# A fused retention and two-layer kernel: the decay of q moved behind the attention, four token blocks loaded ahead of w_in, and a new order of the work

## The chip, the cores and the metric

The kernel runs on one core of a Trainium2 chip. TensorE (PE) multiplies matrices into PSUM, VectorE (DVE) and ScalarE (ACT) do elementwise work, GpSimd (POOL) and SyncE (SP) issue DMA transfers here and compute nothing. The metric is device time in microseconds; three runs of the kernel before took 284.38, 279.27 and 279.20 us, with a median of 279.27 us.

## What is computed

q, k and v have the shape (8 batches, 8 heads, 576 positions, 64), in float32. The attention is a retention: no softmax, but a decay by distance.

```
scores = q @ k.T / sqrt(64)
Dmat   = gamma[h] ** (i - j) for i >= j, else 0        # gamma[h] = 1 - 2 ** (-5 - h)
attn   = (scores * Dmat) @ v
x      = attn, heads side by side                      # (4608, 512)
h      = x @ w_in                                      # (512, 2048)
out    = max(0.01 * h, h) @ w_out                      # (2048, 512)
```

The decay of row i and column j splits into a factor of i, a factor of j and a mask. So the factor of the row may be put on q, or on the row of the result; that of the column goes on v.

## The kernel before

**Blocks and groups.** The 4608 tokens form 36 blocks u of 128 tokens (two chunks of 64) and nine groups g of 512 tokens. A batch has nine chunks, and the decay is counted anew every 256 positions, so a chunk has one of four places in its decay block.

**Attention of one block.** `load` (L348) brings k, q and v as float32 tiles (jobs `ld{u}.1`, `.0` and `.2`; 256 KB each, in two halves where a block crosses a batch). `casts` makes 16-bit copies of them: `ck` is a plain cast (L373). `cq` and `cv` multiply by the decay table, either as one DVE product (L377) or as eight ACT scalings, one for each head (L383). q and k are then turned: for the first eight blocks by PE (`tp`, L413) with a move out of PSUM by DVE or ACT (`yt`, L420), from block 8 on by a transposing DMA on SP's queue (`tr`, L399). `sa` (or `ca`) makes the scores in PSUM (L447), `mk` masks them on DVE (L462), `sb` makes the state sums of k and v (L456), `st` adds them up on DVE (L487 to L493), and `sx` casts the state to 16 bits (L505 to L508). `oa` (or `ca` and `ow`) multiplies masked scores by v and the state by q into the PSUM tile `ot` (L544). `x{u}` casts `ot` into `xT` (L593), the operand of layer 1; in 31 blocks ACT does it and in five DVE.

**The two layers.** Groups 0 and 1 do layer 1 plainly: 16 jobs `h{g}.{f}.{t}` a group (L642, a PSUM bank each) with the leaky relu on ACT (L649). From group 2 on layer 1 is done by seven products of half-size blocks (`a{g}.{n}`, L835) with sums of their results on DVE and copies out of PSUM on ACT or DVE (`cA` L774, `u2` L785, `k5` L788). Layer 2 is done by seven products for all groups (`b{g}`, L913). It needs weight differences that DVE makes once: `wm` of w_out (L688) and `ws` of w_in (L717). PE has four PSUM banks for all these, the pool `acc`.

**What sets the order.** Nothing is scheduled at run time. The string `ORDER` lists every job, and each engine runs its jobs in the order of the list. The table `ENGINE` says which of the castings and copies are DVE's and which ACT's. An item such as `+7@0` stands for seven matmuls of zeros into bank 0 (L982): they compute nothing. They read a tile of zeros, `idle`, that DVE clears at the start (L318).

**The loads.** SP issues k and q of block 0, later k and q from block 12 on and the transposing transfers. All else is issued by POOL, one after the other in the order of the list: the loads, the four blocks of w_in (`wi`, L614, 512 columns each) and the four of w_out (`wo`, L623), which are cast to 16 bits on their way. In the trace, POOL does not issue a transfer before the eighth one ahead of it has landed.

Of the kernel before, what the change touches and what calls it, by code (L numbers as in the profile page):

```python
# [33 lines left out]
class Plan:  # L34
# [52 lines left out]
    for eng, names in {  # L87
        "DVE": """
            ck0 cq0 sx0.0 yt0.0 cq1 sx0.1 cv1 cq2 sx1.0 yt2.1 ck3 cq3 yt3.1 cv3 sx2.1 yt3.0 cq4 cv4 x3 ck5 cq5
            cv5 yt5.1 cq6 sx5 cv6 cq7 ck7 cv7 yt7.0 b0.cA cv8 ck10 sx8.0 cv9 cq9 cq11 cq12 cv10 b1.cA cv13 ck15  # L90
            cv14 cq14 cv15 cq15 sx13.1 sx14 cq16 cv16 cv17 cq17 cq18 a2.3.k5 sx17.0 cv18 sx18 cq19 a3.1.u2 x17
            cv20 ck21 cq21 sx19 a3.2.k5 cq22 cv22 sx20 ck23 cv23 cq23 x20 cv24 cq25 sx23 a4.2.cA cv25 a4.2.u2
            cq26 cq27 cv27 sx25 a5.0.u2 a5.0.k5 cq28 cq29 cv29 ck30 cq30 cv30 ck31 cv31 cq32 sx30 cq33 ck33
            a6.0.cA cv33 cv34 ck34 cq35 cq34 a6.2.cA b5.u2 cv35 a6.3.u2 x32 a7.0.cA x33 a7.0.k5 b5.21 a7.1.cA
            b6.11 b6.u2 a7.3.cA a7.3.u2 a8.0.k5 b7.k5 a8.2.u2 a8.2.k5 b7.21 a8.3.u2 b8.21
        """,
        "ACT": """
            cv0 yt0.1 x0 ck1 ck2 yt1.1 yt1.0 cv2 yt2.0 x1 sx1.1 sx2.0 x2 sx3.0 ck4 sx3.1 yt4.1 yt4.0 ck6 sx4.1
            x4 yt5.0 x5 yt6.0 yt6.1 sx6 yt7.1 sx7 x7 x6 ck8 b0.11 cq8 ck9 b0.u2 cq10 b0.k5 cv11 ck12 sx9 x8 ck11
            cv12 sx10 cq13 b0.21 x9 ck13 sx11 b1.11 sx12 x10 b1.u2 x11 ck14 a2.0.cA b1.k5 a2.0.u2 a2.0.k5 x12  # L100
            a2.1.cA a2.1.u2 x13 a2.1.k5 ck16 ck17 sx15 a2.2.cA a2.2.u2 b1.21 a2.2.k5 sx16 x14 a2.3.cA x15
            a2.3.u2 ck18 b2.cA a3.0.cA b2.11 a3.0.u2 a3.0.k5 a3.1.cA cv19 b2.u2 x16 a3.1.k5 ck19 b2.k5 a3.2.cA
            ck20 cq20 a3.2.u2 cv21 b2.21 ck22 x18 a3.3.cA a3.3.u2 a3.3.k5 x19 b3.cA a4.0.cA b3.11 sx21 ck24
            a4.0.u2 a4.0.k5 cq24 a4.1.cA a4.1.u2 sx22.1 a4.1.k5 x21 b3.u2 ck25 b3.k5 ck26 sx24 a4.2.k5 x22 cv26
            a4.3.cA x23 a4.3.u2 a4.3.k5 ck27 b3.21 a5.0.cA b4.cA ck28 cv28 sx26.0 b4.11 x24 ck29 a5.1.cA a5.1.u2
            a5.1.k5 x25 sx27 sx28 b4.u2 a5.2.cA x26 sx29 b4.k5 a5.2.u2 a5.2.k5 x27 a5.3.cA ck32 a5.3.u2 cv32
            a5.3.k5 cq31 b4.21 x28 x29 sx31.1 a6.0.u2 a6.0.k5 sx32 b5.cA a6.1.cA b5.11 a6.1.u2 x30 a6.1.k5 x31
            a6.2.u2 a6.2.k5 sx33 b5.k5 ck35 a6.3.cA a6.3.k5 sx34 sx35.0 a7.0.u2 b6.cA a7.1.u2 a7.1.k5 a7.2.cA
            a7.2.u2 b6.k5 a7.2.k5 x34 x35 a7.3.k5 a8.0.cA b6.21 a8.0.u2 b7.cA b7.11 a8.1.cA b7.u2 a8.1.k5
            a8.1.u2 a8.2.cA a8.3.cA a8.3.k5 b8.cA b8.u2 b8.k5 b8.11x so8.11x b8.11y  # L110
# [11 lines left out]
    l0.4.256 tp4.0@2 x3 tp5.0@1 yt4.0 st3.1s ld6.1 h0.11.0@0 sx3.1 yt5.0 ld6.2 h0.9.0@2 yt4.1 ck5 cv4 ld7.0
    h0.10.0@1 l0.9.0 tp5.1@3 ld7.2 l0.10.0 ca4 sb4 h0.4.384@2 mk4 ld7.1 cv5 h0.8.0@1 l0.4.384 st4.1 ld8.2 yt5.1 ow4
    sb5 x4 h0.15.0@2 st5.0 sx4.1 st5.1 l0.11.0 h0.14.0@3 sx5 ld8.1 ca5 l0.14.0 cq6 l0.8.0 ld9.2 ws3.1 h0.13.0@0 mk5
    ld9.1 h0.0.128@3 l0.13.0 cv6 wo2 h0.0.384@1 l0.0.128 ld10.2 l0.15.0 tp6.0@0 h0.0.256@3 ck6 yt6.0 ld10.1 tp6.1@2
    l0.0.384 ow5 sb6 wo0 x5 h0.12.0@0 st6.0s yt6.1 ld8.0 h1.0.0@1 cv7 l0.0.256 cq7 ld9.0 h1.2.0@2 l1.0.0 ck7 st6.1
# [88 lines left out]
def kernel(  # L215
# [150 lines left out]
    def casts(u):  # L366
# [5 lines left out]
        def ck():  # L372
            copies[ke](out=by_half(t[:, 1]), in_=in_halves(t32[u, 1][:]))  # L373
# [680 lines left out]
```

## Time and profile before

| | |
|---|---|
| median of three runs | 279.27 us |
| the profiled execution | 281.72 us |
| its span, first to last instruction | 279.9 us |
| granted TensorE clock over the span | 1.000 |
| busy: PE, DVE, ACT, POOL | 269.7, 229.9, 206.6, 72.4 us |
| first layer-1 matmul, first layer-2 matmul, last matmul begins its run | 18.75, 50.80, 275.30 us |

The span is what the profiler saw between the first and the last instruction; 1.8 us of the profiled execution lie around it. In the views a row of a timeline has its start, its length, the engine, the line and the tiles, a count, and in brackets how long the engine stood idle before it and what ended that. A row of a window has the busy time of each engine with the number of its instructions, the clock, the busy share of the DMA engines and the GB/s that they moved. Zero matmuls count as busy.

### The profile page before, as it was taken

What the parts mean: (1) busy time and instruction counts of PE and PEld (TensorE: products, weight loads), DVE (VectorE), ACT (ScalarE), POOL (GpSimd) and SP (SyncE); (2) the same over time, 40 slices, a digit from 0 to 9 for tenths busy, and PEclk for the clock granted to TensorE, in tenths of its full rate; (3) what the DMA queues carried; (4) which work ended last, traced back from release to release, by engine and by line L of the source; (5) the groups of instructions that cost most, each with busy time, mean ns of one, the idle gap of its engine ahead of it and who ended that gap; (6) DMA issues with size and microseconds to landing.
All of it is one profiled execution on the core that took longest, in us unless ns stands there. A gap on an engine that the chain in (4) does not pass through costs nothing.

```text
span 279.9 us, 10117 instructions
## 1 busy us (share of the span) xinstructions
PE 269.7 (96%) x4337; PEld 224.7 (80%) x4337; DVE 229.9 (82%) x431; ACT 206.6 (74%) x459; POOL 72.4 (26%) x92
## 2 busy tenths in 40 slices
PE   7878999899999999999999999999999999999994
...
GB/s 220 238 207 222 275 253 244 260 218 219 213 239 226 213 305 253 155 211 273 277 201 262 187 220 187 148 260 214 21 148 51 68 3 2 152 0 0 77 96 131
DMA packets 94364, 50.04 MB, mean 179 GB/s; under 512 B 83312, under 2 KB 88560, under 8 KB 94320
## 3 DMA queue, kind: packets, MB, share of 16 engines
...
q14 instruction: 10, 0.08, 0.1%
HBM read 36.81 MB, written 9.44 MB: 165 GB/s over the span
## 4 chain that ended last, share of the span: by engine, by line
PE 84%; DMA 11%; POOL 1%; issue 1%; DVE 1%; ACT 0%; POOLq 0%; DVEq 0%
PE acc L913 37%; PE acc L835 32%; PE acc L642 6%; DMA w_in<-in_moe_w_in_dram 6%; PE ot L544 4%; DMA w_out<-in_moe_w_out_dram 4%; PE sc L456 2%; DMA t<-in_k_dram 2%; PE sc L447 2%; POOL t L348 1%; PE sc L913 1%; PE acc L413 0%; DVE w_mix L688 0%; DVE w_out L688 0%; ACT st L505 0%
## 5 line engine op out<-in xcount | busy, mean ns | idle before, releaser
L913 PEld LDWEIGHTS <-gt 128*128 128x128 f16 x720 | 69.8, 98 | 9.5 <-DMA w_out<-in_moe_w_out_dram 0.8
L348 POOL DMA_DIRECT2D t<-in_v_dram x40 | 34.4, 860 | 101.1 <-DVE v L377 63.3
L913 PE MATMUL acc<-w_out,gt 128*128 128x256 f16 x416 | 51.5, 273 | 0.9 <-DMA w_out<-in_moe_w_out_dram 0.9
L835 PEld LDWEIGHTS <-w_in 128*128 128x128 f16 x448 | 42.4, 98 | 5.6
L855 ACT ACTIVATE gt<-acc 128x512 f16<-128x512 f32 x56 | 33.4, 599 | 16.6 <-PE acc L835 16.4
L863 ACT ACTIVATE gt<-sum 128x512 f16<-128x512 f32 x56 | 34.7, 632 | 4.7 <-DVE sum L859 4.7
L913 PE MATMUL acc<-w_mix,gt 128*128 128x256 f16 x288 | 36.2, 273 | 0.0
L835 PEld LDWEIGHTS <-w_sum 128*128 128x128 f16 x336 | 32.2, 98 | 4.1
L835 PE MATMUL acc<-xs,w_sum 128*128 128x256 f16 x224 | 33.6, 273 | 0.0
L835 PE MATMUL acc<-xT,w_in 128*128 128x256 f16 x224 | 33.5, 273 | 0.0
L835 PE MATMUL acc<-xs,w_in 128*128 128x256 f16 x224 | 33.4, 273 | 0.0
L732 POOL DMA_DIRECT2D out_dram<-osb x16 | 11.5, 718 | 83.9 <-ACT acc L774 38.5
L642 PE MATMUL acc<-xT,w_in 128*128 128x256 f16 (+2 forms) x272 | 30.8, 266 | 0.9 <-DMA w_in<-in_moe_w_in_dram 0.7
L913 PEld LDWEIGHTS <-mix 128*128 128x128 f16 x288 | 28.1, 98 | 3.6 <-issue 0.3
L642 PEld LDWEIGHTS <-w_in 128*128 128x128 f16 x272 | 22.0, 98 | 6.0 <-DMA w_in<-in_moe_w_in_dram 0.8
L462 DVE TENSOR_TENSOR s<-sc,cs 128x512 f16<-128x512 f32 x36 | 24.6, 684 | 2.7 <-PE sc L447 1.8
L859 DVE TENSOR_TENSOR sum<-acc,k 128x512 f32<-128x512 f32 x28 | 19.2, 686 | 7.8 <-PE acc L835 5.7
L649 ACT ACTIVATE gt<-acc 128x512 f16<-128x512 f32 x32 | 18.2, 600 | 7.6 <-PE acc L642 7.4
L377 DVE TENSOR_TENSOR qk<-t,cs 128x512 f16<-128x512 f32 x30 | 20.5, 684 | 3.4 <-DMA t<-in_q_dram 3.4
L788 ACT COPY k<-acc 128x512 f32<-128x512 f32 x29 | 16.9, 588 | 7.8 <-PE acc L913 4.0
L593 ACT CAST xT<-ot 128x512 f16<-128x512 f32 x31 | 18.2, 588 | 5.2 <-PE ot L544 5.2
L383 ACT ACTIVATE v<-t,cs 128x64 f16<-128x64 f32 x72 | 18.2, 341 | 3.5 <-DMA t<-in_v_dram 2.9
...
## 6 DMA issues: line engine op xcount, KB each, us to landing
...
```

Of the source, the lines that this page charges most:

```text
L348: engine[eng].dma_start(out=t[CH * j : CH * j + rows], in_=(q, k, v)[x][b, :, CH * w : CH * w + rows, :].rearrange("h t d -> t h d"),)
L377: engine[e].tensor_tensor(out=view[0](out), in0=view[1](t32[u, 2 * x][:]), in1=view[1](decay(u, x)), op=MUL)
L383: nc.scalar.mul(out=out[:, at(h), :], in_=t32[u, 2 * x][:, h, :], mul=tab_sb[:, w, x, h : h + 1])
L462: landed[u] = nc.vector.tensor_tensor(out=s[:], in0=sc[:, :, 0], in1=mask_sb.unsqueeze(1).unsqueeze(1).to_broadcast([P, 2, NP, CH]), op=MUL,)
L593: moved[u] = copies[xe](out=x_of(u).rearrange("q c (j t) -> q j c t", j=2), in_=at)
L642: nc.tensor.matmul(out=a[:, n, :], lhsT=w_in16[:, c, (f0 + n) * P : (f0 + n + 1) * P], rhs=x[:, c, t0 : t0 + nt], start=(n == 0 and c == 0 ...
L649: nc.scalar.activation(out=y[:, f0 : f0 + nf, t0 : t0 + nt], in_=a[:], func=mybir.ActivationFunctionType.Lrelu)
L835: nc.tensor.matmul(out=r[:, f, :], lhsT=w[:, c, (2 * n + f) * P : (2 * n + f + 1) * P], rhs=rhs[:, c, :], start=fresh and c == 0 and f == ...
L855: w = op(what, "ACT", lambda: nc.scalar.activation(out=to(), in_=r[:], func=lr), after, [y], [r])
L859: what, "DVE", lambda: nc.vector.tensor_tensor(out=s[:], in0=r[:], in1=plus[:], op=ADD),
L863: f"l{g}.{n}.{what}", "ACT", lambda: nc.scalar.activation(out=to(), in_=s[:], func=lr), [j], [y],
L913: nc.tensor.matmul(out=(r[tb] if isinstance(r, tuple) else r)[:, tb, :], lhsT=lhs[n]()[:, f, tb * P : (tb + 1) * P], rhs=rhs[n][:, f, :], ...
```

## The change

What it does, by parts:

1. `cq` becomes a plain cast, like `ck`. The row factor comes in at the end: `x{u}` is always a DVE product of `ot` and a table `q_tab`, written to `xT`. `q_tab` is made on the chip at the start by four DVE products (`tb0` to `tb3`) from two short tables, and the table of constants holds the decay of v alone.
2. POOL issues ten loads before the first block of w_in where it issued seven, so that k, q and v of blocks 0 to 3 stand ahead of it. The second and third blocks follow sooner on the first. One load fewer stands ahead of the last block of w_out.
3. `cq8` gets a dependency on `wm2.1`, a weight difference that needs the last block of w_out. The first transposing DMA on SP reads what `cq8` writes.
4. The zeros are read from a part of `w_mix`; the tile `idle` is gone. There are 36 zero matmuls for 33, in other places: 9, 6, 2, 2, 2, 4, 3, 3 and 5, where there were 13, 4, 3, 2, 7, 2 and 2.
5. The state's running sum has a pool of its own with three buffers; the scaling of it works in place.
6. `ORDER` and `ENGINE` are new. On DVE there are now 18 casts of k (12 before), 12 of q, 27 products of v (27), 19 state casts (15), 4 `cA` (8), 7 `u2` (9) and 8 `k5` (7); ACT has the rest. On PE, all attention of blocks 0 to 3 stands ahead of the first layer-1 job; before, that job stood ahead of the outputs of block 2 and the scores of block 3.

```diff
@@ CFG
+    fp=3,
@@ def decay / q_table
-    def decay(u, x):
+    def decay(u):
         w = kinds.index((place(2 * u), place(2 * u + 1)))
-        return tab_sb[:, w, x, :].unsqueeze(2).to_broadcast([P, H, D])
+        return tab_sb[:, w, :].unsqueeze(2).to_broadcast([P, H, D])
+
+    steep = []
+
+    def q_table():
+        for a in range(NB):
+            def run(a=a):
+                nb = CH // FINE
+                nc.vector.tensor_tensor(
+                    out=q_tab[:, a].rearrange("p c (b r) -> p c b r", b=nb),
+                    in0=fine_sb.unsqueeze(2).to_broadcast([P, NP, nb, FINE]),
+                    in1=coarse_sb[:, :, a].unsqueeze(3).to_broadcast([P, NP, nb, FINE]), op=MUL,
+                )
+
+            steep.append(add(f"tb{a}", "DVE", run))
@@ def casts
-        def cq():
-            scaled(t[:, 0], 0, qe, lambda h: 2 * (h % NP) + h // NP, (by_half, in_halves))
...
-        cast[u, 0] = add(f"cq{u}", qe, cq, [loaded[u, 0]], [t], [t32[u, 0]])
+        cast[u, 0] = add(f"cq{u}", qe, lambda: plain(0, qe), [loaded[u, 0]], [t], [t32[u, 0]])
@@ def inner
-                    tmp = t_pool.tile([P, NP, CH], FP, name="stmp")
-                    nc.vector.tensor_tensor(out=tmp, in0=x, in1=before[0][:, before[1]], op=ADD)
+                    nc.vector.tensor_tensor(out=to, in0=x, in1=before[0][:, before[1]], op=ADD)
                     nc.vector.tensor_tensor(
-                        out=to, in0=tmp, in1=gblk_sb.unsqueeze(2).to_broadcast([P, NP, CH]), op=MUL
+                        out=to, in0=to, in1=gblk_sb.unsqueeze(2).to_broadcast([P, NP, CH]), op=MUL
                     )
@@ def outer_copy
-            moved[u] = copies[xe](out=x_of(u).rearrange("q c (j t) -> q j c t", j=2), in_=at)
-
-        copied[u] = add(f"x{u}", xe, cp, [j], [xT[u // 4]], [ot_banks])
+            by_place = (
+                q_tab[:, p0 : p0 + 1].to_broadcast([P, 2, NP, CH]) if p0 == p1
+                else q_tab[:, p0 : p1 + 1 : p1 - p0] if p0 < p1
+                else q_tab[:, p0 : (p1 - 1 if p1 else None) : p1 - p0]
+            )
+            moved[u] = nc.vector.tensor_tensor(
+                out=x_of(u).rearrange("q c (j t) -> q j c t", j=2), in0=at, in1=by_place, op=MUL
+            )
+
+        copied[u] = add(f"x{u}", "DVE", cp, [j] + [steep[p] for p in sorted({p0, p1})], [xT[u // 4]], [ot_banks])
@@ at the start, and behind sum_weights()
-    idle = const_pool.tile([P, TOK], F16, name="idle")
+    idle = w_mix[:, 2, 0:2].rearrange("p f n -> p (f n)")
+    cast[CFG["turned"], 0].after.append(mixed_w[2, 1])
```

**POOL, from its seventh transfer on.** `t_0`, `t_1` and `t_2` are tiles of q, k and v, `w_in` a block of w_in; `x2` is a pair of halves or of like transfers. Before:

```order
L348 DMA t_2_165<-in_v_dram 128x8x64
L614 DMA w_in_123<-in_moe_w_in_dram 128x4x512
L348 DMA t_1_220<-in_k_dram 128x8x64
L348 DMA t_0_226<-in_q_dram 128x8x64
L348 DMA t_1_260<-in_k_dram 64x8x64 x2
L348 DMA t_2_293<-in_v_dram 128x8x64
L348 DMA t_0_326<-in_q_dram 64x8x64 x2
L348 DMA t_0_445<-in_q_dram 128x8x64
L614 DMA w_in_123<-in_moe_w_in_dram 128x4x512
```

and of the change, from the same place:

```order
L363 DMA t_2_221<-in_v_dram 128x8x64
L363 DMA t_2_223<-in_v_dram 128x8x64
L363 DMA t_1_262<-in_k_dram 128x8x64
L363 DMA t_0_312<-in_q_dram 128x8x64
L641 DMA w_in_124<-in_moe_w_in_dram 128x4x512
L363 DMA t_0_324<-in_q_dram 64x8x64 x2
L641 DMA w_in_124<-in_moe_w_in_dram 128x4x512
L363 DMA t_1_359<-in_k_dram 64x8x64 x2
L641 DMA w_in_124<-in_moe_w_in_dram 128x4x512
```

Three loads have moved ahead of the first block of w_in, and the second and third blocks come one pair of halves behind the one before; they had eight and four transfers between, each half counted.

**DVE, from the clearing of the zeros on.** `sc` holds scores and state sums in PSUM, `cs` the table of constants, `s` a masked score or a state, `st` a state in 16 bits. Before:

```order
L318 MEMSET idle 128x256
L373 CAST qk_147<-t_1_135 128x2x4x64
L377 TENSOR_TENSOR qk_147<-t_0_139,cs 128x2x4x64
L377 TENSOR_TENSOR qk_163<-t_0_141,cs 128x2x4x64
L487 COPY s_222<-sc 128x256
L420 COPY qkT<-acc 128x512
L377 TENSOR_TENSOR qk_228<-t_0_149,cs 128x2x4x64
L377 TENSOR_TENSOR v_258<-t_2_152,cs 128x512
L489 TENSOR_TENSOR s_222<-sc,s_222 128x256
L508 CAST st_265<-s_222 128x256
L462 TENSOR_TENSOR s_291<-sc,cs 128x512
```

and of the change, two stretches of the same engine's order, the second one ending with block 3's mask and the x products of blocks 2 and 3:

```order
L333 MEMSET w_mix 128x256
L381 TENSOR_TENSOR q_tab<-cs 128x256 x4
L406 TENSOR_TENSOR v_183<-t_2_139,cs 128x512
L402 CAST qk_188<-t_1_143 128x2x4x64
L508 COPY s_208<-sc 128x256
L510 TENSOR_TENSOR s_208<-sc,s_208 128x256
...
L618 TENSOR_TENSOR xT<-ot,q_tab 128x2x4x64
L510 TENSOR_TENSOR s_483<-sc,s_410 128x256
L483 TENSOR_TENSOR s_485<-sc,cs 128x512
L618 TENSOR_TENSOR xT<-ot,q_tab 128x2x4x64
L483 TENSOR_TENSOR s_550<-sc,cs 128x512
L618 TENSOR_TENSOR xT<-ot,q_tab 128x2x4x64 x2
```

The q products have left the start, the four table products have come ahead of all else, and four x products follow each other closely.

**SP, its first transfers.** `qkT` is the turned q and k, and the transposing rows read blocks 8 and 9. Before:

```order
L348 DMA t_1_135<-in_k_dram 128x8x64
L348 DMA t_0_139<-in_q_dram 128x8x64
L399 DMA_TRANSPOSE qkT<-qk_1048 128x8x128
L348 DMA t_1_1417<-in_k_dram 128x8x64
L348 DMA t_0_1429<-in_q_dram 128x8x64
L399 DMA_TRANSPOSE qkT<-qk_1115 128x8x128
```

and of the change:

```order
L363 DMA t_0_137<-in_q_dram 128x8x64
L363 DMA t_1_141<-in_k_dram 128x8x64
L420 DMA_TRANSPOSE qkT<-qk_1111 128x8x128
L363 DMA t_1_1471<-in_k_dram 128x8x64
L363 DMA t_0_1501<-in_q_dram 128x8x64
L420 DMA_TRANSPOSE qkT<-qk_1106 128x8x128
```

The order is the same but for q and k of block 0; what has changed is that `qk_1111`, the tile of block 8, gets its q only behind the weight difference, and the loads of block 12 stand behind the transfer that reads it.

More of the change, by code (lines that the diff above doesn't have):

```diff
@@ L100 @@
[L100 to L109, printed above, removed]
@@ L122 @@
[L122 to L126, printed above, removed]
@@ new lines @@
+    b1.p5.1 b1.p7.0 ld15.0 x11 xs2.0 xs2.1 a2.0.11 m1.3.1 b1.k5 a2.0.p5.0@2 a2.0.p6.0 mk12 ld16.0 b1.p3.0 a2.0.k5
+    a2.0.p3.0 ld17.0 cv16 xs2.2 a2.0.u2 st13.1 b1.p3.1 ld16.1 a2.0.p7.0 ck14 xs2.3 a2.0.12 cv14 cq14 b1.12 b1.p7.1
+    ow12 sb14 a2.0.22 ld18.2 b1.22 l2.0.22 ca13 a2.1.p1.0@2 ck15 st14.0 b1.p4.0 cq15 cq16 a2.1.cA@0 a2.0.p4.0
+    a2.1.p6.0 l2.0.12 st14.1 mk13 cv15 tr14 a2.0.21 x12 tr15 a2.1.p2.0 a2.1.p5.0@1 sx13.1 a2.1.u2 b1.p4.1 a2.1.p7.0
+    a2.1.k5 a2.1.p3.0 b1.21 a2.2.p1.0@3 sb15 ws4.1 a2.1.22 sx14 a2.1.11 ow13 ca14 a2.1.12 a2.2.p5.0@1 ck16 a2.2.cA@2
@@ L211 @@
+    m8.1.1 b8.p5.1 m8.2.1 m8.3.1 so7.1 m8.3.0 b8.p6.0 b8.k5 b8.p6.1 b8.u2 b8.p2.0 b8.p7.0 b8.11x b8.p7.1 b8.22
+    b8.p3.0 so8.11x so8.22 b8.p3.1 b8.p4.0 b8.12 b8.p4.1 so8.12 b8.21 b8.p2.1 so8.21 b8.11y so8.11y
 """
@@ L248 @@
     kinds = sorted({(place(2 * n), place(2 * n + 1)) for n in range(NU)})
-    tab = np.zeros((P, len(kinds), 2, H))
+    tab = np.zeros((P, len(kinds), H))
     for w, at in enumerate(kinds):
         r = np.concatenate([CH * a + np.arange(CH) for a in at])[:, None] - BLK / 2
-        tab[:, w, 0] = gamma[None, :] ** r * scale
-        tab[:, w, 1] = gamma[None, :] ** (-r)
+        tab[:, w] = gamma[None, :] ** (-r)
+    NB, FINE = BLK // CH, 16
+    fine, coarse = np.zeros((P, NP, FINE)), np.zeros((P, NP, BLK // FINE))
+    for c in range(NP):
+        for oo in range(2):
+            rows = slice(CH * oo, CH * oo + CH)
+            fine[rows, c] = gamma[2 * c + oo] ** np.arange(FINE)
+            coarse[rows, c] = gamma[2 * c + oo] ** (FINE * np.arange(BLK // FINE) - BLK / 2) * scale
     s_idx = np.arange(P) % CH
@@ L275 @@
     a_pool = pool("ap", CFG["ap"])
+    f_pool = pool("fp", CFG["fp"])
     c_pool = pool("cp", CFG["cp"])
@@ L286 @@
     n_pool = pool("np", 4)
-    t_pool = pool("tp", 1)
     sc_pool = pool("scp", 1, PSUM)
@@ L370, in casts, with plain, cv @@
         ke, qe, ve = by(f"ck{u}", "ACT"), by(f"cq{u}", "DVE"), by(f"cv{u}", "DVE")
-        def ck():
-            copies[ke](out=by_half(t[:, 1]), in_=in_halves(t32[u, 1][:]))
-        def scaled(out, x, e, at, view):
-            if e != "ACT":
-                engine[e].tensor_tensor(
-                    out=view[0](out), in0=view[1](t32[u, 2 * x][:]), in1=view[1](decay(u, x)), op=MUL
-                )
+        def plain(x, e):
+            copies[e](out=by_half(t[:, x]), in_=in_halves(t32[u, x][:]))
+        def cv():
+            if ve != "ACT":
+                engine[ve].tensor_tensor(out=s[:], in0=t32[u, 2][:], in1=decay(u), op=MUL)
                 return
```

229 lines of the change are left out of this document (120 added, 109 removed), and 12 rows, old and new, of the table loads.

## The prediction

> **What bounds the kernel now.** I read the page's busy times and slices first, then a table of windows over the start, then the PE timeline and the chain of waits at the places where PE is not full.
>
> ```profile
> span 279.9 us, 10117 instructions
> PE 269.7 (96%) x4337; PEld 224.7 (80%) x4337; DVE 229.9 (82%) x431; ACT 206.6 (74%) x459; POOL 72.4 (26%) x92
> ...
> PE   7878999899999999999999999999999999999994
> ...
> PE 84%; DMA 11%; POOL 1%; issue 1%; DVE 1%; ACT 0%; POOLq 0%; DVEq 0%
> ```
>
> PE is busy for 96% of the span, and PE holds 84% of the chain. The only other large holder is DMA, 11%, and it sits in the first quarter. So time can be won where PE idles or multiplies zeros, in the first 63 us, and lost anywhere an engine begins to starve PE. The windows (PE, PEld, DVE, ACT, POOL, clock, DMA share, GB/s) show where:
>
> ```profile
> 0.00:7.00 7.00, 5.58 (x13) 1.79 (x13) 1.58 (x5) 2.70 (x8) 5.90 (x11) 1.00 0.78 221
> 7.00:14.00 7.00, 6.11 (x124) 3.70 (x125) 5.56 (x13) 5.76 (x18) 6.73 (x9) 1.00 1.04 237
> 14.00:21.00 7.00, 4.95 (x94) 2.92 (x93) 3.83 (x10) 3.13 (x7) 3.32 (x5) 1.00 0.80 206
> 21.00:28.00 7.00, 5.89 (x139) 3.96 (x138) 5.32 (x12) 3.94 (x8) 5.29 (x7) 1.00 1.06 222
> 28.00:35.00 7.00, 7.00 (x134) 4.10 (x132) 4.04 (x10) 4.29 (x9) 4.37 (x6) 1.00 1.15 274
> 42.00:49.00 7.00, 6.86 (x155) 5.72 (x154) 5.28 (x11) 5.91 (x12) 3.99 (x6) 1.00 1.12 245
> 49.00:56.00 7.00, 6.13 (x92) 5.11 (x90) 5.64 (x11) 4.53 (x10) 3.91 (x5) 1.00 1.16 259
> 56.00:63.00 7.00, 6.85 (x64) 6.00 (x62) 6.20 (x12) 4.06 (x12) 0.89 (x1) 1.00 1.17 219
> 71.00:218.00 147.00, 147.00 (x2611) 126.88 (x2610) 139.32 (x268) 127.30 (x284) 27.44 (x34) 1.00 0.94 203
> ```
>
> From 28 us PE is full, but for 0.14 + 0.87 + 0.15 = 1.16 us between 42 and 63. From 71 to 218 it is full without a gap, with DVE at 139.32 of 147. Before 28 us it idles 5.5 us, and part of what counts as busy is zeros. The PE timeline, the POOL timeline and the chain tell what those early stretches wait for:
>
> ```profile
> 1.23 5.58 PE L982 MATMUL acc<-idle 128*128 128x512 f16 x13 [1.23 <-DVE idle L318]
> 18.51 0.40 PE L413 MATMUL acc<-ident,qk 128*128 128x128 f16 x4 [1.77 <-DVE qk L373]
> 18.75 1.04 PE L642 MATMUL acc<-xT,w_in 128*128 128x256 f16 x8
> 19.62 0.59 PE L982 MATMUL acc<-idle 128*128 128x512 f16 x2
> 24.13 0.32 PE L544 MATMUL ot<-s,v 64*64 64x64 f16 x16
> 24.28 0.61 PE L544 MATMUL ot<-qkT,st 64*64 64x64 f16 x16
> 26.10 2.76 PE L642 MATMUL acc<-xT,w_in 128*128 128x512 f16 x12 [0.66 <-DMA w_in<-in_moe_w_in_dram]
> 50.80 1.05 PE L913 MATMUL acc<-w_out,gt 128*128 128x256 f16 x8 [0.67 <-DMA w_out<-in_moe_w_out_dram]
> 55.53 1.03 PE L913 MATMUL acc<-w_out,gt 128*128 128x256 f16 x8 [0.19 <-DMA w_out<-in_moe_w_out_dram]
> ```
>
> ```profile
> 17.33 0.90 POOL L348 DMA_DIRECT2D t<-in_q_dram  x1 [3.60 <-DMA w_in<-in_moe_w_in_dram]
> ...
> 18.03 0.43 DVE L373 CAST qk<-t 128x512 f16<-128x512 f32 x1 [2.98 <-DMA t<-in_k_dram]
> ```
>
> ```profile
> 7.57 9.22 DMA w_in<-in_moe_w_in_dram
> 18.29 7.77 DMA w_in<-in_moe_w_in_dram
> 48.99 10.53 DMA w_out<-in_moe_w_out_dram
> ```
>
> The first w_in block is issued at 7.57, ahead of block 3's q and k, and lands at 16.79. POOL waits 3.60 us for it before it issues more, so the queue of transfers runs dry (share 0.80, 206 GB/s at 14 to 21). Block 3's k lands only at 18, and blocks 2 and 3 finish their attention between matmuls of layer 1. The second w_in block lands at 26.06, and PE starts on it at 26.10. That is the last start-up wait.
>
> **The change, part by part.** *Start.* With four blocks loaded before w_in, the order has all their attention ahead of the first layer-1 job. It is then bounded by DVE. DVE's prices:
>
> ```profile
> L462 DVE TENSOR_TENSOR s<-sc,cs 128x512 f16<-128x512 f32 x36 | 24.6, 684 | 2.7 <-PE sc L447 1.8 <-PE sc L456 0.9
> ...
> L377 DVE TENSOR_TENSOR qk<-t,cs 128x512 f16<-128x512 f32 x30 | 20.5, 684 | 3.4 <-DMA t<-in_q_dram 3.4
> ...
> L489 DVE TENSOR_TENSOR s<-sc,s 128x256 f32<-128x256 f32 x40 | 16.7, 419 | 3.1 <-PE sc L456 2.2 <-PE sc L447 0.8
> ...
> L785 DVE COPY u<-acc 128x512 f32<-128x512 f32 x9 | 6.2, 686 | 2.7 <-PE acc L835 2.7
> ...
> L373 DVE CAST qk<-t 128x512 f16<-128x512 f32 x12 | 5.2, 444 | 6.8 <-DMA t<-in_k_dram 6.8
> L508 DVE CAST st<-s 128x256 f16<-128x256 f32 x7 | 2.5, 352 | 0.0
> ```
>
> Up to block 3's mask DVE now does four products for the q table (4 x 0.419), three scalings of v (3 x 0.684), one cast of k (0.444), eight state sums and two moves of transposed blocks (10 x 0.419), four state casts (4 x 0.352), four masks and two x products (6 x 0.684): 13.9 us; where a form is new or has no row here, the price is that of the nearest row of its size. It can start near 4.3, since the table lies on chip before the product that reads it at 5.15:
>
> ```profile
> 3.93 0.43 DVE L373 CAST qk<-t 128x512 f16<-128x512 f32 x1 [2.76 <-DMA t<-in_k_dram]
> 5.15 0.69 DVE L377 TENSOR_TENSOR qk<-t,cs 128x512 f16<-128x512 f32 x1 [0.80 <-DMA t<-in_q_dram]
> ...
> 30.17 0.68 DVE L377 TENSOR_TENSOR v<-t,cs 128x512 f16<-128x512 f32 x1
> 30.77 0.42 DVE L487 COPY s<-sc 128x256 f32<-128x256 f32 x1
> ```
>
> 4.3 + 13.9 = 18.2 with neither gap nor overlap. The last two rows show starts 0.60 apart for 0.68 of duration, so these 28 instructions overlap by some 2 us, down to 16.0; waits for PE and for transfers add some of it back. I take 17.8. PE's last step of block 3 (the rows at 24.13 and 24.28, 0.8 together) and five zero matmuls (0.59 for two, so about 1.2) follow: the first layer-1 job starts at 19.8. Then PE lacks, against its state at 26.10 before, three layer-1 jobs (0.87 each; the row at 18.75 has 1.04 with its tail) and three transposes (0.25 each): 3.35 us. It stands at 23.1 where it stood at 26.10: **3.0 us sooner**. Bounds: 4.8 (DVE done at 16.0) and nothing (the first w_in block 3 us later than 19.8). With three more loads ahead on POOL, 256 KB at some 259 GB/s each (1.0 us), that block lands near 16.79 + 3.0 = 19.8, just in time, so I keep the middle.
>
> *w_out.* The waits of 0.67 and 0.19 and the hops beside them are the 1.16 us above. They go, and the 3.0 us stay won, if w_out comes sooner by 3.0 + 1.2 = 4.2 us. The last block landed at 48.99 + 10.53 = 59.52. Two things bring it forward. At the mean of the full windows (274, 245 and 259, so 259 GB/s), what the windows from 7 to 28 moved, (237 + 206 + 222) x 7, is 18.0 us of work in 21: 3.0 us of hole that back-to-back loads can close. And 34 loads instead of 35 stand ahead of it: 1.0 us. Both: 4.0 us, landing at 55.5; the second alone: 58.5. I take three quarters of the hole, 56.3, 0.8 to 1.2 us short of all that is wanted at that last block; but 3.5 us more of layer 1 now stands ahead of layer 2's first job, which covers the blocks that land before. I count **1.2 us** of gain with bounds of -1.8 (w_out only 1.0 sooner eats most of the 3.0) and 2.3 (less is lost also in the small steps between).
>
> *DVE and ACT after 71 us.* Before, x was mostly ACT's:
>
> ```profile
> L593 ACT CAST xT<-ot 128x512 f16<-128x512 f32 x31 | 18.2, 588 | 5.2 <-PE ot L544 5.2
> ...
> L593 DVE CAST xT<-ot 128x512 f16<-128x512 f32 x5 | 3.4, 684 | 0.3 <-PE ot L544 0.3
> ```
>
> Between groups 1 and 6 of layer 2 (71 to 218 us) the tables give DVE 23 x products where it had 2 casts of x (+21 x 0.684 = 14.4), 8 q casts where it had 20 q products (3.6 - 13.7 = -10.1), five more k casts (+2.2), three more state casts (+1.3), and fewer v scalings (-1.4) and copies of accumulators (-2.8): +3.6 us. 139.3 + 3.6 = 142.9 of 147: still below PE, price nothing. A product out of PSUM with a broadcast table is what the mask does at 684 ns, and a cast of ot on DVE costs 684 too, so I price x at 684; bounds are 588 and 1368 (a copy and a product one after the other). ACT, at 127.3 of 147, gives up 18.2 us of x casts, takes over q casts in their place, and stays below. The cover is PE's own work; without it the 3.6 us would be paid.
>
> *Held transfer.* Cast 8 of q now waits for a mix of w_out's last block, so the first transposing transfer and two loads behind it on SP start after 56.3 + about 1.5 = 57.8. Before, that transfer started at 57.90:
>
> ```profile
> 57.90 1.94 SPq L399 DMA_TRANSPOSE qkT<-qk  x1
> ```
>
> Price nothing; if w_out lands at 59.5 it is 3 us late, and so are blocks 12 and 13, needed from group 3's layer 1 on, after 100 us. *Zero matmuls* go from 33 to 36 and fill time in which PE has nothing else; only the last five lie in the sum above. The smaller table, the pool of three and the padding change no time that I can see.
>
> Sum: 3.0 + 1.2 = 4.2 us. The profiled execution took 281.72 (span 279.9 and 1.8 around it), so 277.5 in such an execution; the median of the three runs, 279.27, is 2.45 lower, which gives **275.0 us**.
>
> **The rivals.** (1) *The transfers set the start of layer 2* (0.20): for it, the queue is full from 28 us on, and more loads come ahead of w_in. w_out then lands only 1.0 us sooner, PE waits for it, and 1.2 us are won: 278.0. (2) *All of the hole closes* and DVE's chain ends at 16.0 (0.14): 4.8 + 1.7 = 6.5, so 272.8. (3) *DVE becomes the bound, slower* (0.06): if each x product costs 1.37 us, 23 of them add 15.7 to 142.9, 158.6 for a stretch of 147: 11.6 lost less 4.2 won, 286.7. It decides from 4.1 / 23 = 0.18 us over 0.684 on. The mask's row speaks against it. (4) *DVE at 97% is late in small pieces* (0.08): its 3.6 us are paid in full, 278.6. For it: PE has four accumulators of one bank each, so that it waits soon for a late copy. (5) *More casts on DVE hold up POOL's transfers* (0.03): if a cast of k or q on DVE stops POOL for its 0.444 us, the nine that stand before w_out's landing, for five before, bring w_out 1.8 us later: 276.8. The cast at 18.03 ran inside the issue at 17.33, which took 0.90 us like others, so little speaks for it. The Trainium skill ("SBUF — State Buffer", section "Who interferes with whom") has a rule for this: DVE copies and casts can take a port pair that GpSimd needs, and a transfer issued from GpSimd then waits for its descriptors. By that rule this change would pay, since q turns from product to cast; by the pair of rows above it would not.
>
> **How the numbers follow.** The forecast has 0.49; with 273.6 to 276.6 as its own range. The range of 272.3 to 278.6 takes in rivals 1, 2, 4 and 5 and leaves out the DVE-bound case and the tails. A measurement of this kernel can tell about 2%, 5.6 us, from no change: faster is below 273.7, slower above 284.9. Rival 2 and the forecast's lower edge give 0.21 for faster, rival 3 gives 0.05 for slower, and 0.74 stays within.
>
> **What would show it.** Right: the first layer-1 matmul near 19.8 with no layer-1 work ahead of block 3's last attention step, no POOL wait of 3 us between 14 and 18, PE full from 23 to 24 us on, waits for w_out of nearly nothing, DVE near 97% from 67 to 214, x products at 684 ns. Wrong: a wait for w_in or w_out of over 1 us on PE, x products over 0.86 us, or gaps in PE after 71 us.

## The result and the profile after

The changed kernel takes 291.09 us (median of four, 289.81 to 293.84), the kernel before 279.24. The ratio is 1.044, with a 95% interval of 1.035 to 1.053: slower, where 275.0 us were forecast. Where executions of one kernel lie more than 1.5% apart, the ratios here use the faster ones alone, so that a median can lie above what its ratio gives.

The page of the changed kernel, its rows as in the page of before:

```profile
span 289.0 us, 10088 instructions
PE 272.7 (94%) x4340; PEld 226.9 (79%) x4340; DVE 236.8 (82%) x453; ACT 192.3 (67%) x399; POOL 72.7 (25%) x92
...
PE   8889999997699999995999999899999999999995
...
PEclk9999999999699999999999999999999999999999
...
PE 76%; DMA 11%; DVE 7%; ACT 2%; issue 2%; POOL 1%; DVEq 0%; POOLq 0%; ACTq 0%
```

From the fourth slice on (21.7 us) PE's row is full, as forecast. Two holes have appeared where there was none, near 72 and near 130 us, and behind the first one the granted clock is down. DVE's share of the chain of waits has gone from 1% to 7%. The windows show the same holes: from 71 to 218 us, where PE had no gap, it now lacks 8 us. DVE is less busy in that stretch than before, but the stretch also holds less work; over the whole kernel it is busy for 236.8 us, before 229.9.

```profile
14.00:21.00 7.00, 5.70 (x162) 3.51 (x148) 5.44 (x11) 3.54 (x8) 4.20 (x6) 1.00 1.14 218
21.00:28.00 7.00, 6.83 (x70) 4.86 (x68) 3.07 (x7) 4.04 (x8) 5.52 (x8) 1.00 1.15 263
49.00:56.00 7.00, 7.00 (x66) 6.26 (x65) 6.39 (x12) 4.97 (x10) 2.06 (x3) 1.00 1.15 276
71.00:218.00 147.00, 138.89 (x2432) 118.82 (x2432) 130.32 (x257) 109.21 (x233) 25.65 (x32) 0.98 0.91 198
```

The PE timeline names what ended the holes. The rows with L940 between 74 and 82 are runs of eight matmuls, or two such runs (x16): at full clock a run of eight takes 0.87 us from its start to the next.

```profile
20.62 2.80 PE L669 MATMUL acc<-xT,w_in 128*128 128x256 f16 x32
69.05 1.04 PE L940 MATMUL acc<-w_out,gt 128*128 128x256 f16 x8
74.51 0.32 PE L564 MATMUL ot<-qkT,st 64*64 64x64 f16 x6 [3.99 <-DMA qkT<-qk]
74.99 1.89 PE L940 MATMUL acc<-w_out,gt 128*128 128x256 f16 x8
76.67 1.92 PE L940 MATMUL acc<-w_out,mix 128*128 128x256 f16 x8
78.38 3.00 PE L940 MATMUL acc<-w_out,gt 128*128 128x256 f16 x16
81.21 1.04 PE L940 MATMUL acc<-w_mix,mix 128*128 128x256 f16 x8
105.17 1.91 PE L940 MATMUL acc<-w_out,gt 128*128 128x256 f16 x16
133.27 0.25 PE L564 MATMUL ot<-qkT,st 64*64 64x64 f16 x6 [3.30 <-DMA qkT<-qk]
137.09 1.91 PE L940 MATMUL acc<-w_out,gt 128*128 128x256 f16 x16
```

At 74.51 and 133.27 PE had waited for a transposing transfer, of block 10 and of block 20; the rows are the first matmuls of `ca10` and `ca20`. From 74.99 to 81.21 four runs take 6.2 us where they need 3.5: 2.7 us, in which the windows give half the clock:

```profile
72.00:76.00 4.00, 1.49 (x29) 1.15 (x29) 1.24 (x3) 0.00 (x0) 0.01 (x1) 0.72 1.21 204
76.00:80.00 4.00, 4.00 (x21) 2.86 (x19) 2.76 (x6) 3.01 (x10) 0.23 (x1) 0.50 1.23 171
```

SP's queue and the chain of waits show the transfers: block 8's starts where it did in the trace of before (57.85 for 57.90), block 10's is the first of the three at 66.64 and takes 7.83 us, block 20's takes 8.16.

```profile
57.85 1.32 SPq L420 DMA_TRANSPOSE qkT<-qk  x1
...
66.64 7.40 SPq L420 DMA_TRANSPOSE qkT<-qk  x3
```

```profile
66.64 7.83 DMA qkT<-qk
125.06 8.16 DMA qkT<-qk
```

### The profile page after: what moved, and what is told of

Same layout as the page of the kernel before. It is cut to its first block, busy times and chain, and to the rows that moved or that the text cites. A ratio compares the mean times of both kernels' runs of the same rounds, so it can differ in the third digit from the quotient of the medians.

```text
span 289.0 us, 10088 instructions
## 1 busy us (share of the span) xinstructions
PE 272.7 (94%) x4340; PEld 226.9 (79%) x4340; DVE 236.8 (82%) x453; ACT 192.3 (67%) x399; POOL 72.7 (25%) x92
## 4 chain that ended last, share of the span: by engine, by line
PE 76%; DMA 11%; DVE 7%; ACT 2%; issue 2%; POOL 1%; DVEq 0%; POOLq 0%; ACTq 0%
PE acc L940 34%; PE acc L862 26%; PE acc L669 8%; DMA qkT<-qk 6%; DMA t<-in_q_dram 4%; PE ot L564 3%; DMA t<-in_k_dram 2%; PE sc L468 1%; PE sc L477 1%; PE sc L940 1%; DVE sum L886 1%; POOL t L363 1%; DVE mix L916 1%; DVE v L406 1%; DVE s L510 1%
## 5 line engine op out<-in xcount | busy, mean ns | idle before, releaser
L940 PEld LDWEIGHTS <-gt 128*128 128x128 f16 x720 | 70.9, 99 | 10.0 <-DVE gt L916 0.8
L940 PE MATMUL acc<-w_out,gt 128*128 128x256 f16 x416 | 53.4, 279 | 0.0
L940 PE MATMUL acc<-w_mix,gt 128*128 128x256 f16 x288 | 36.2, 273 | 0.5 <-DVE gt L916 0.5
L890 ACT ACTIVATE gt<-sum 128x512 f16<-128x512 f32 x56 | 33.2, 628 | 1.1 <-DVE sum L886 1.0
L862 PE MATMUL acc<-xs,w_in 128*128 128x256 f16 x224 | 32.4, 273 | 0.0
L940 PEld LDWEIGHTS <-mix 128*128 128x128 f16 x288 | 28.5, 99 | 3.9
L402 ACT CAST qk<-t 128x512 f16<-128x512 f32 x42 | 25.6, 619 | 6.3 <-DMA t<-in_q_dram 3.8
L801 ACT COPY acc<-acc 128x512 f32<-128x512 f32 x32 | 18.4, 576 | 13.1 <-PE acc L940 7.0
L618 DVE TENSOR_TENSOR xT<-ot,q_tab 128x512 f16<-128x512 f32 x36 | 24.4, 681 | 1.6 <-PE ot L564 1.6
L812 ACT COPY u<-acc 128x512 f32<-128x512 f32 x30 | 17.5, 588 | 11.3 <-PE acc L940 6.5
```

The source lines that it names most:

```text
L402: copies[e](out=by_half(t[:, x]), in_=in_halves(t32[u, x][:]))
L618: moved[u] = nc.vector.tensor_tensor(out=x_of(u).rearrange("q c (j t) -> q j c t", j=2), in0=at, in1=by_place, op=MUL)
L801: copies[ce](out=B[:], in_=A[:])
L812: op("u2", ue, lambda: copies[ue](out=u2[:], in_=B[:]), [done["6"]], [u2], [B])
L862: nc.tensor.matmul(out=r[:, f, :], lhsT=w[:, c, (2 * n + f) * P : (2 * n + f + 1) * P], rhs=rhs[:, c, :], start=fresh and c == 0 and f == ...
L890: f"l{g}.{n}.{what}", "ACT", lambda: nc.scalar.activation(out=to(), in_=s[:], func=lr), [j], [y],
```

## The experiments

The first theory was this. PE now asks for blocks 10 and 20 before their transposing transfers are in, and each wait costs its length and a few microseconds of half clock behind it. Its rivals were the held-back first transfer, a full set of DMA engines, and DVE. In the expectations theory 2 is the held transfer (or the chain of transfers as a whole); theory 3 is DVE in the first of them and the full DMA engines from e9 on.

**Block 10's scores later on PE** (e1_late10):

```diff
- m1.0.0 ca10 b1.p1.1 ... b1.p5.0@0 m1.1.1 mk10 b1.p2.0 b1.p2.1 ld14.1 b1.p6.0 ow10
+ m1.0.0 b1.p1.1 ... b1.p5.0@0 m1.1.1 b1.p2.0 b1.p2.1 ld14.1 b1.p6.0 ca10 mk10 ... ow10
```

> The scores of block 10 (ca10), its mask and its outputs stand about 4 us of PE work later, behind b1.p6.0; nothing else moves. Theory 1 (PE's order asks for block 10 before its transposing transfer is in, and the clock falls because PE then idles): the wait of 3.99 us and the 2.7 us at a low clock go, so 291.1 - 6.7 = 284.4 us (283 to 286), clock 1.00 from 72 to 84 us. Theory 2 (the whole chain of transposing transfers is late because of the held cq8): the wait moves on to block 11 or 12 and less than 2 us is won, 289 to 291. Theory 3 (DVE bounds the middle of the kernel): no change, 291.

Measured: 286.37 us, ratio 1.026 (1.023 to 1.030). The wait at block 10 and the low clock behind it are gone, but 4.7 us are won instead of 6.7: there are new waits of 0.3 to 0.7 us behind the move, and at block 20 PE waits 3.84 us and the clock falls, which it had not done there. Theory 1 holds for the place and not for the sum.

**The wait filled with matmuls** (e2_filled10):

```diff
- m1.0.0 ca10
+ m1.0.0 +16@0 ca10
```

> Sixteen matmuls that compute nothing (some 3.7 us) stand ahead of ca10, where PE waited 3.99 us. They shorten no wait. If the clock falls because PE stands idle there, it now stays at 1.00 and the 2.7 us lost after the wait come back: 288.4 us (287.5 to 289.5). If the clock falls for another reason, the time stays at 291.

Measured: 284.18 us, ratio 1.013 (1.011 to 1.015). The clock is 1.00 from 70 to 90 us. The traced execution took 287.73 us and another one 288.91, 2 to 3 us less than the change, as expected if the clock falls because PE stands idle; block 20's wait and a low clock behind it remained in the trace. The three fastest executions, on which the ratio rests, had a mean clock of 1.00 and were 7 to 8 us faster than the change. Why those did not dip at block 20 has not been settled.

**The hold undone** (e3_free8):

```diff
-    cast[CFG["turned"], 0].after.append(mixed_w[2, 1])
- b0.p1.1 sx8.0 wm2.1 cq8 wm0.1
+ m0.1.1 l1.10.256 cq8 wm2.0
```

> The hold is undone: cq8 has no dependency on w_out and stands on DVE ahead of wm2.0, some 7 us earlier. Theory 2 (the hold makes the transposing transfers late): the first one starts near 51 instead of 57.85, that of block 10 lands before PE asks for it at 70.5, and the wait and the low clock go: 284.4 us, less 0 to 2 us if w_out now lands later. Theory 1 without the hold as its origin (transfer of block 10 slowed by stores and loads beside it): it still lands after 72 and 288 us or more remain.

Measured: 286.08 us (282.0 to 287.9), ratio 1.014 (1.008 to 1.021). In the traced execution block 10's wait is gone; block 20's is 4.01 us, with a low clock behind it. So the second wait does not come from the hold. That the hold has a part in the first one is not shown by this trace alone: e14 below has no hold and the wait, e5 has the hold and hardly any wait.

**Block 10's transfer ahead of block 13's loads** (e4_turn_first):

```diff
- tr9 ... ld13.1 ... ld13.0 ... tr10
+ tr9 ... tr10 ld13.1 ld13.0
```

> On SP the transposing transfer of block 10 stands ahead of the k and q loads of block 13 instead of behind them; the hold stays. Theory 1: it is issued near 63.8 instead of 66.64 and, at 4 to 5 us, lands by 69, before PE asks at 70.5: 284.4 us. If its 7.8 us come from what runs beside it and not from its place in the queue, it lands near 71.5 and a wait of 1 us and some low clock stay: 287 to 289.

Measured: 288.92 us, with executions from 283.2 to 293.6, too far apart for a ratio. Block 10's wait is gone, and PE waits at block 12 (1.01 us), for copies at 78 and 88 us, and at block 20 (3.34 us). The wait moved along the queue.

**Block 20 later, and with the free cq8** (e5_late20, e6_free8_late20):

```diff
- ow19 ck22 ca20 a3.2.p7.0 ... b3.p1.0@0
+ ow19 ck22 a3.2.p7.0 ... b3.p1.0@0 ca20 mk20
```

> The hold and block 10 are as in the changed kernel; the scores of block 20 and their mask stand 4.4 us of PE work later, behind b3.p1.0. Theory 1 (each wait for a transposing transfer costs its own length and the low clock that follows): 3.3 and about 2.6 us go, 291.1 - 5.9 = 285.2 us (284 to 287); the first wait, at block 10, stays. Theory 2 (the transfers as a chain are behind, and PE meets the next one): a wait of 2 us or more at block 21 or 22, 288 or more.

> Both: cq8 without the hold and earlier, and block 20's scores behind b3.p1.0. Theory 1: no wait for a transposing transfer is left; from the run with the free cq8 (profile 283.0 us in span, 4.2 us of wait at block 20 and 2.5 at the low clock) that leaves a span of 276.5 and a time of about 278 us, between 276.5 and 279, so at or below the 279.5 of the kernel before. If the start's gain of 3 us is real it must show here. Theory 2: 281 or more, with waits at other blocks.

Measured: 286.97 us, ratio 1.026 (1.020 to 1.032), and 290.45 us, ratio 1.034 (1.026 to 1.042). The first won 4 of the 5.9 us, but not by its edit alone. In its trace (285.74 us) block 10's wait is 0.35 us too, though nothing ahead of it differs from the change: that transfer took 4.80 us here, for 7.83. With neither wait and a mean clock of 0.999, this execution is still 6 us longer than the kernel before; PE loses most of them in many waits of 0.3 to 0.9 us, most of them for copies and sums of ACT and DVE. The second, which should have been the best, has a median as high as the change's. In its trace, at 286.88 us its fastest execution, PE waits at blocks 11 and 12 (0.70 and 0.90 us) with the clock at 0.58 from 80 to 84 us, and 1.90 us for a product of DVE near 180 us. Theory 1, taken as two waits that can be removed one by one, falls here.

**One store later; stores cut; the same cut in the kernel before** (e7_free8_store, e9_less_stored, e10_before_less_stored):

```diff
# e7, on top of e3
- ld25.2 ... tr20 so2.0 ... ld26.2
+ ld25.2 ... tr20 ... ld26.2 so2.0
# e9 and e10, groups 0 to 4
-            nc.gpsimd.dma_start(out=out[r0 : r0 + HT, :].rearrange("(t p) d -> p t d", p=P), in_=o[:])
+                nc.gpsimd.dma_start(out=out[r0 : r0 + P, 0:64], in_=o[:, 0, 0:64])
```

> cq8 free as before, block 20 asked for as early as in the changed kernel, but the output store that POOL issues while block 20's transposing transfer is under way (so2.0) is issued later, behind the v load of block 26. If the 8 to 9 us of that transfer come from the store beside it, it lands in 4 to 5 us and the wait is gone: 277 to 279 us. If they come from the loads and the other transposing transfers on SP's own queue, it stays near 8 us: 284 to 286 us.

> The changed kernel, with the output stores of groups 0 to 4 cut to a sixteenth (32 KB of 512 KB each; the other rows and columns of those groups are left out of the output). All else stays. Theory 3 (from 60 us on the DMA engines are full, and a transposing transfer that runs beside a 512 KB store or a load takes 8 to 10 us instead of 3 to 5): the waits at blocks 10 and 20 shrink to under 1 us each and the clock stays up: 280 to 283 us. Theory 1 (PE's order asks too soon whatever runs beside): 288 to 291 us.

> The same cut of the stores in the kernel before, as a control. It waits for no transfer after 60 us, so every theory expects 279.0 to 279.6 us; a gain of over 1 us would say that the cut saves something else than waits for transposing transfers.

Measured: e7 283.55 us, ratio 1.011 (1.004 to 1.018), with block 20's transfer at 7.41 us for 8.89 and its wait at 2.53 for 4.01. e9 284.02 us, ratio 1.009 (1.004 to 1.014), so 7 us less than the change. e10 279.78, ratio 1.001 (0.998 to 1.004). Cutting the stores is worth nothing to the kernel before and more than half of the loss to the changed one. The PE timeline of e9 has one wait of over 0.5 us left after 50 us, and the window from 71 to 218 lacks 2.3 us where the change lacked 8.1:

```profile
72.85 0.32 PE L564 MATMUL ot<-qkT,st 64*64 64x64 f16 x6 [3.23 <-DMA qkT<-qk]
```

```profile
71.00:218.00 147.00, 144.71 (x2545) 124.74 (x2545) 137.02 (x270) 112.99 (x241) 24.09 (x31) 0.99 0.76 166
```

The share of the DMA engines is 0.76 there, for 0.91. Block 10's wait is hardly shorter (its transfer takes 7.23 us), so what slows that transfer is not the stores; block 20's takes 5.31 us, for 8.16.

**The loads alone** (e8_before_loads), the kernel before with three loads ahead of w_in:

```diff
- cq1 ld2.2 +13@3 tp1.0@0 wi1 ... ld3.1 ... ld3.0 ... ld4.1 ... ld3.2
+ cq1 ld2.2 +13@3 tp1.0@0 ... ld3.1 ... ld3.0 ... ld3.2 wi1 ld4.1
```

> The kernel before, with one part of the change alone: the loads of block 3 stand ahead of the first block of w_in on POOL's queue, and PE's order is the old one. If the start's gain comes from the loads alone, PE is full 2 to 3 us sooner and the time is 277 us. If it needs PE's order too (the first layer-1 job now waits for w_in, landing near 19.8, ahead of attention that could run), the time is within 1 us of 279.5 us or 1 us longer.

Measured: 282.07 us, ratio 1.007 (1.003 to 1.011). Nothing is won. One execution took 279.18 us with a mean clock of 1.00; the others had 0.99 and 281.6 to 283.4. The trace shows why, in the window of 4 us behind a wait of 1.81 us for w_in (PE idle for 1.9 of the 4 us before):

```profile
16.00:20.00 4.00, 2.13 (x23) 1.29 (x17) 1.80 (x4) 1.08 (x2) 0.73 (x2) 0.98 1.10 256
20.00:24.00 4.00, 3.88 (x81) 2.67 (x80) 1.62 (x3) 1.05 (x4) 3.91 (x5) 0.59 0.94 227
```

**The decay alone** (e11_old_order): the plain cast of q, the table and x as a DVE product, in the old order, with the old loads.

```diff
- ck0 ld2.0 cq0
+ tb0 tb1 tb2 tb3 ck0 ld2.0 cq0        # all cq on ACT, all x on DVE, no hold
```

> One part of the change alone: q only cast (all casts of q on ACT), the table products, and x as a DVE product, in the order, the loads and the other engine choices of the kernel before; nothing held back. If the decay's move is harmless, DVE has 31 x products for 30 q products, ACT 31 x casts less and 36 q casts for 6 sets of scalings and no more: 278.5 to 281 us. If part of the 12 us comes from it (x late behind DVE's queue, so that layer 1 waits), 284 us or more.

Measured: 288.69 us, ratio 1.029 (1.022 to 1.036), in the traced execution 290.2 us with a span of 288.4. With all casts of q on ACT, this part by itself costs 8 to 9 us in the old order. Layer 2's second group starts at 74.2 us, 5.7 later than in the kernel before, with a low clock from 7 to 14 us; and from 71 to 218 PE lacks 3.3 us in many small pieces while DVE has room:

```profile
7.00:14.00 7.00, 4.57 (x55) 2.34 (x55) 2.00 (x5) 6.06 (x18) 6.70 (x9) 0.76 1.07 260
...
71.00:218.00 147.00, 143.69 (x2558) 122.56 (x2557) 134.47 (x257) 118.97 (x253) 26.67 (x33) 1.00 0.92 201
```

**The start given away** (e12_start_later):

```diff
- oa3 +5@2 h0.6.0@0
+ oa3 +17@2 h0.6.0@0
```

> The changed kernel with twelve zero matmuls more ahead of the first layer-1 job: PE's work starts 3.0 us later, so what the start won is given away. If the transfers set the pace after 60 us (theories 1 and 3), the waits at blocks 10 and 20 shrink by as much and the time stays at 291 us or falls, down to 286 us where the clock then holds. If PE's own work sets it, 294 us.

Measured: 286.93 us, ratio 1.023 (1.017 to 1.030). PE starts layer 1 at 23.0 us for 20.6, and the kernel is 4 us faster. Block 10's wait is 2.20 us for 3.99, block 20's is gone. So PE's own work does not set the pace of the changed kernel there; a later start even helps it.

**Both kernels traced again, and three moves together** (e13_before_again, e15_after_again, e14_three_moves: cq8 as in e3, the store as in e7, and ca20 behind a3.2.p3.0).

> The kernel before, unchanged, traced a second time. The trace behind the prediction had a span of 279.9 us where nearly all other executions have 277.3 to 278.0. If that one execution was long in its start, this trace shows PE 2 to 3 us sooner at the first layer-1 jobs and at layer 2 (68.7 instead of 71.1 us), and the start of the changed kernel is then worth about 1 us and not 3. If the difference lies elsewhere, the start is as it was and the 3 us were real.

> The changed kernel, unchanged, traced a second time: waits of 2 to 4 us at blocks 10 and 20, each followed by some 4 us at about half the clock, and 289 to 294 us. If the waits are elsewhere in this execution, the places named so far are chance, and only their sum (PE ahead of its transfers) is a property of the order.

> The changed kernel with cq8 free and early, the store so2.0 behind the v load of block 26, and block 20's scores 1.7 us of PE work later. Theory 3: the wait at block 10 is gone with the free cq8 and the one at block 20 has shrunk to under 1 us: a span of 278 to 280, 280 to 282 us where the clock holds. If it stays above 283, waits for transfers turn up wherever PE is early, and no single move repairs it.

Measured: e13 279.12 us with a span of 277.3, as expected of it. In its POOL and PE timelines the wait for w_in is 2.64 us instead of 3.60, the first zeros take 4.44 us instead of 5.58, and layer 2's second group starts at 68.52 instead of 71.12; the other rows give the same place in later groups, and SP's transfers for blocks 10 and 20 with PE's use of them:

```profile
1.23 4.44 PE L982 MATMUL acc<-idle 128*128 128x512 f16 x13 [1.23 <-DVE idle L318]
...
68.52 1.91 PE L913 MATMUL acc<-w_out,gt 128*128 128x256 f16 x16
71.39 0.26 PE L544 MATMUL ot<-qkT,st 64*64 64x64 f16 x10
98.05 1.91 PE L913 MATMUL acc<-w_out,gt 128*128 128x256 f16 x16
125.20 0.30 PE L544 MATMUL ot<-qkT,st 64*64 64x64 f16 x16
126.45 1.91 PE L913 MATMUL acc<-w_out,gt 128*128 128x256 f16 x16
```

```profile
65.38 6.93 SPq L399 DMA_TRANSPOSE qkT<-qk  x3
...
117.06 3.13 SPq L399 DMA_TRANSPOSE qkT<-qk  x1
```

```profile
16.41 0.89 POOL L348 DMA_DIRECT2D t<-in_q_dram  x1 [2.64 <-DMA w_in<-in_moe_w_in_dram]
```

So the trace that the prediction was made from was long in its start by 2.6 us. e15 took 291.75 us; its waits are the same two, and here each is followed by a window at 0.57:

```profile
73.16 0.25 PE L564 MATMUL ot<-qkT,st 64*64 64x64 f16 x6 [3.44 <-DMA qkT<-qk]
...
131.16 0.25 PE L564 MATMUL ot<-qkT,st 64*64 64x64 f16 x6 [3.79 <-DMA qkT<-qk]
```

```profile
74.00:78.00 4.00, 4.00 (x24) 2.94 (x23) 3.26 (x7) 3.01 (x10) 0.33 (x1) 0.57 1.14 331
...
132.00:136.00 4.00, 4.00 (x24) 2.93 (x23) 2.94 (x6) 1.79 (x4) 0.00 (x0) 0.57 1.16 302
```

e14 took 287.65 us, ratio 1.028 (1.024 to 1.031): above 283, so these three moves together do not repair it. With cq8 free the first transposing transfer starts at 49.13, beside w_out, and takes 13.0 us where the change's takes 4.5. The last block of w_out takes 13.14 us (12.11 in the change, but 13.12 in e5, which has no such transfer beside it); PE waits for it, and for block 10 all the same:

```profile
57.24 1.03 PE L940 MATMUL acc<-w_out,gt 128*128 128x256 f16 x8 [1.29 <-DMA w_out<-in_moe_w_out_dram]
73.69 0.25 PE L564 MATMUL ot<-qkT,st 64*64 64x64 f16 x6 [3.17 <-DMA qkT<-qk]
```

## Why the prediction was wrong

**Where the time went.** The same place in the second, third and later groups of layer 2, each with the same work before it from group 2 on, kernel before (e13) against the change:

| layer 2 of group | before, us | changed, us | changed later by |
|---|---|---|---|
| 1 (0.87 us more of layer 1 done before it in the change) | 68.52 | 69.05 | 0.5, so 0.3 sooner in work |
| 2 | 98.05 | 105.17 | 7.1 |
| 3 | 126.45 | 137.09 | 10.6 |

The spans differ by 11.7 us (289.0 and 277.3), so nine tenths of the loss lie between 69 and 137 us. The waits are 3.99 and 3.30, the low clock 2.7: 10.0 of the 10.9 us that the table shows between groups 1 and 3. The rest there is small waits, and another microsecond is lost after group 3. These places are those of the traced execution: e15 has the same two waits, e5 neither of them.

**The start: right in mechanism, and mis-sized.** The forecast had the first layer-1 job at 19.8 us; it is at 20.62, and at 20.17 in e15. From there to 63 us PE lacks 0.17 us before 28 and 0.46 between 42 and 49, and of POOL's wait of 3.60 us for w_in 1.66 is left. But "3.0 us sooner" was taken against one execution that was 2.6 us longer up to layer 2's second group than e13. The median of the runs, 2.45 us below that execution, stood in the prediction, and was taken off at the end as if it lay evenly over the span; it lay in the very term that the change removes. Against e13 the start wins 0.3 us in the traced execution and 1.1 in e15.

**w_out: the landing right, the gain not there.** The forecast had the last block at 56.3 us; it lands at 55.89, and PE waits for it nowhere (7.00 of 7 us from 49 to 56). But in e13, with the old order, it lands at 55.07: it came no sooner, and that the forecast meets the measured time is luck. The 1.16 us of waits belonged to that execution too: in e13 PE idles 0.14 us between 42 and 63.

**DVE: the prices right.** x is a product at 681 ns, as the mask's row said:

```profile
L618 DVE TENSOR_TENSOR xT<-ot,q_tab 128x512 f16<-128x512 f32 x36 | 24.4, 681 | 1.6 <-PE ot L564 1.6
```

That rules out rival 3. From group 2 to group 6 of layer 2 DVE has 113.2 us of work in e9 and 111.1 in e13, so about 2 us more, and is not the bound. Rival 4 shows in part: DVE's 7% of the chain, and a wait of PE for a DVE product (L916) near 184 us, 0.53 us in the first trace and 1.85 in e15; e12 has 1.01 us for an x product near 122 us. That the move of the decay costs nothing was a step without ground: e11 shows 8 to 9 us for it in the old order. Of what that is made, beyond the later start and the many small waits, has not been settled. In the new order's steady part it costs little: from group 2 to group 6 of layer 2, e9 needs 118.0 us (101.29 to 219.30) and the kernel before 117.4 (98.05 to 215.48).

**The step that failed: "Held transfer. Price nothing".** The time itself came true, 57.8 us forecast and 57.85 measured, but the row beside it, 57.90, is again from the long execution: in e13 the transfer starts at 55.97, so the change starts it 1.9 us later and not at the same time. The prediction then asked when blocks 12 and 13 are needed and not when blocks 8 to 11 are. It took two things for unchanged, without a reason: the room between the issue of a transposing transfer and its use, and the time that the transfer takes. The rows that had to be read are SP's issue and PE's use, for each block; "before" is e13:

| block | before: issue, landed, use, room | changed: issue, asked for, room, landed |
|---|---|---|
| 10 | 65.38, 69.3, 71.39, 6.0 us | 66.64, 70.5, 3.9 us, 74.5 |
| 20 | 117.06, 124.2, 125.20, 8.1 us | 125.06, 130.0, 4.9 us, 133.2 |

What the transfers took, from issue to landing, is in the view of the tile qkT. Block 10's, in e13 and in the change:

```profile
DMA to landing us min/median/max: 3.9/3.9/3.9
```

```profile
DMA to landing us min/median/max: 7.8/7.8/7.8
```

Block 20's, in e13 and in the change:

```profile
DMA to landing us min/median/max: 7.1/7.1/7.1
```

```profile
DMA to landing us min/median/max: 8.2/8.2/8.2
```

And all 28, in the first trace of before and in the change (shortest, median, longest):

```profile
DMA to landing us min/median/max: 2.7/4.6/7.8
```

```profile
DMA to landing us min/median/max: 2.7/4.5/10.1
```

At block 10 the room shrank by 2.1 us: the issue is 1.26 later than in e13, the use 0.87 sooner. That alone would have cost next to nothing, since a transfer of 3.9 us would have landed at 70.6, as PE asks for it. The wait of 3.99 us comes with the transfer's doubled time. At block 20 it is the other way round: a transfer of 7.1 us as in e13 would have waited 2.2 of the 3.30 us in the room of 4.9. Of the 3.2 us of room lost there, some 2.6 lie in the new `ORDER` itself: six layer-1 products (24 matmuls at 0.109 us) stand ahead of ca20 in the old list and behind it in the new one. The forecast had no term for this. No rival had such a wait in it. The last part of the prediction named gaps in PE after 71 us as what would make it wrong, and they are what did.

**What set the landing.** e12 (start given away: 4 us faster) and e9 against e10 (stores cut: 7 us faster here, nothing there) show that between 69 and 137 us the transfers set the pace of the changed kernel; e5 shows that small waits take their place where both are missing. e4, e6 and e14 show that to move one transfer or one use hands the wait on. For block 20 the stores are a part of the cause. Block 10's transfer took 3.2 to 4.1 us in all five traces of the old order and 4.7 to 7.8 in the twelve of the new one. What makes it longer, and why e5 has 4.8 with the same work ahead of it, stays open.

**The clock.** It was in no term of the sum. The first trace shows it at half for some 7 us around a wait of 3.99 us, e15 for some 3.5 us behind each of its two; e2 removes the first dip by filling the wait with matmuls, and block 10's transfer still lands at 73.2 us. The Trainium skill ("TensorE: Matmul & The Clock Gate", section "Part 1: The HAM clock gate (the "warmup" mystery)") says that PE runs at half clock after an idle window of about 3.4 us, and that this window runs freely. The runs agree for the waits of 3.4 to 4.0 us. For shorter ones they do not: the clock also fell behind 3.17 us (e14), 2.20 (e12) and 1.81 (e8), and it stayed up behind 3.30 us at block 20 in the first trace and 2.53 in e7. So the length of one wait does not decide it, and what does has not been settled.
